# Tying later weight conversions behind one another, and reordering early loads, in an attention and two-FFN kernel

## The chip, the cores and the metric

The kernel runs on one core of a Trainium2 chip. The metric is the device time of one execution in microseconds (us); the time given for a kernel is the median of several runs. A core has a matmul engine (PE, with its weight loads shown as PEld), three engines for element-wise work (DVE, ACT and POOL), and SP, which here only issues DMAs. Every engine works through its own list of instructions in the order in which the program wrote it, and waits on semaphores for what other engines or DMAs bring. PE's clock has two levels, 1.2 and 2.4 GHz; the profile gives the granted share of the higher one.

## The reference

What is computed is windowed attention with a linear bias, followed by two feed-forward networks, all in float32:

```python
def _attn_ref(q, k, v):                       # (4, 8, 576, 64) each
    scores = scale * np.matmul(q, k.transpose(0, 1, 3, 2))
    bias = slopes[:, None, None] * (-np.abs(rel))[None]
    mask = (rel >= 0) & (rel < 128)
    scores = np.where(mask, scores + bias[None], -1e9)
    scores = scores - np.max(scores, axis=-1, keepdims=True)
    attn = np.exp(scores)
    attn = attn / (np.sum(attn, axis=-1, keepdims=True) + 1e-09)
    return np.matmul(attn, v)

def _moe_ref(x, w_in, w_out):                 # 2304 x 512, 512 x 2048, 2048 x 512
    h = x @ w_in
    return (h * (1.0 / (1.0 + np.exp(-1.702 * h)))) @ w_out

def _moe2_ref(x, w_gate, w_val, w_out):       # 512 x 1536 twice, 1536 x 512
    g = x @ w_gate
    return (g * (1.0 / (1.0 + np.exp(-g))) * (x @ w_val)) @ w_out
```

The output of each stage is the input of the next. The weights arrive as 64-bit words.

## The kernel before

The 2304 tokens form 18 tiles of 128, in five blocks of 4, 2, 4, 4 and 4 tiles. For each block the kernel runs attention (scores, row minima, exponentials, normalisation, transposes, values), then the first network (W1, that is `w_in` and `w_out`, in 16 chunks of 128 hidden features), and writes the result to DRAM. The second network follows for all tokens at 538 us of the span.

**W1.** Chunk c comes by two DMAs of 512 KB (`load_w`, L186) into a tile `wraw`, which holds 64-bit words. `split_steps` turns it into a high and a low float32 part in five instructions: ACT scales the upper words into `cv` (L197), DVE shifts the lower words in place (L199), DVE joins both (L201), ACT copies the high part into `wt` (L206), and DVE subtracts to get the low part (L208). L199 depends on nothing but the landing of its chunk. `cv` has two buffers.

A matmul by W1 is three: high by high, high by low, low by high (L554 to L556). For chunk f of block j, `h_steps` makes `hp` (12 matmuls), then ACT's tanh (L575), DVE's product (L577), ACT's high part `gh` (L583) and DVE's low part `gl` (L585); `y_part` multiplies these by the chunk's `w_out`, 12 matmuls into four banks `y`.

**What sets the order.** The first part of the program is written out by hand: `PLAN` is a list of tokens, and inside `tc.manual_schedule` PE, DVE, ACT and POOL take the instructions in that order. It covers attention of blocks 0 and 1, W1's chunks 0 to 8 (tokens w0 to w4, in the order 0, 1, 2, 5, 3, 4, 6, 7, 8) and chunks 0 to 7 of block 0's first network. What follows the plan is placed by a scheduler, which may move an instruction ahead into the planned stretch where it depends on nothing there. After the plan block 1 goes through all 16 chunks, then block 0 through chunks 8 to 15; chunks 9 to 15 are converted by `split_next`, called from the loop over `seq`, one chunk for every two of block 1's.

**Loads.** All are issued by SP in one order: q, k and v of block 0 (`load_full`), chunks 0 to 7 of W1, q, k, v of the first two head pairs of block 1 (`load_pair`, tiles `qr`, `kr`, `vr`), then, as buffers come free, chunks 8 to 15 and the other pairs. Chunks 12 to 15 take over buffers that block 1's attention frees. The raw words of `w_gate` and the other weights of the second network are fetched by `fetch` (L250) and prepared in the gaps of the first network (`preparation`, `in_order`); `in_order` queues each of these steps behind the instructions held in `marks`, by an edge of order within one engine, with no semaphore.

Tile names carry numbers in the lists of instructions below: `wraw_132`, `135`, `138`, `141`, `144`, `147` are chunks 0 to 5, `548`, `551`, `554`, `557` chunks 8 to 11, and `1041`, `1044`, `1047`, `1050` chunks 12 to 15. Chunks 6 and 7 are `150` and `153` before, `164` and `167` after.

## Time and profile before

| what | value |
|---|---|
| median of 3 runs | 934.69 us (931.45 to 935.67) |
| the profiled execution, its own time | 936.22 us |
| its span in the profile | 934.3 us |
| mean granted clock of PE | 0.989 |
| PE, DVE, ACT, POOL busy | 904.1, 676.8, 452.2, 117.3 us |

The span runs from the first to the last record of the profile; 1.9 us of the execution's time lie around it. A row of a timeline gives start, duration, engine, line, operation, output and input; a bracket at its end gives the idle time of that engine just before, and what ended it. A row of a table of windows gives, for each engine, the time that it was busy in that stretch and, behind x, the number of its instructions. Matmul durations overlap, so the spacing of starts is what a matmul costs.

### The profile page before, as it was taken

What the parts mean: (1) busy time and instruction counts of PE and PEld (TensorE: products, weight loads), DVE (VectorE), ACT (ScalarE), POOL (GpSimd) and SP (SyncE); (2) the same over time, 40 slices, a digit from 0 to 9 for tenths busy, and PEclk for the clock granted to TensorE, in tenths of its full rate; (3) what the DMA queues carried; (4) which work ended last, traced back from release to release, by engine and by line L of the source; (5) the groups of instructions that cost most, each with busy time, mean ns of one, the idle gap of its engine ahead of it and who ended that gap; (6) DMA issues with size and microseconds to landing.
All of it is one profiled execution on the core that took longest, in us unless ns stands there. A gap on an engine that the chain in (4) does not pass through costs nothing.

```text
span 934.3 us, 15603 instructions
## 1 busy us (share of the span) xinstructions
PE 904.1 (97%) x5572; PEld 801.1 (86%) x5572; DVE 676.8 (72%) x1716; ACT 452.2 (48%) x1052; POOL 117.3 (13%) x221
## 2 busy tenths in 40 slices
PE   6779999999999999999999999999999999999998
PEld 4456898777777877778888899999999999999998
DVE  7668685676676667766647668899976679866777
ACT  5645474554465446554434445545444435344331
POOL 4632102331233003230000000000000000000000
PEclk9979999999999999999999999999999999999999
DMA  9943311344654445434563587999897667887763
GB/s 327 343 178 105 119 47 34 115 159 140 217 196 161 155 173 186 139 125 174 201 234 114 214 325 282 319 351 340 323 342 283 247 238 242 281 298 249 262 243 136
DMA packets 72461, 201.30 MB, mean 215 GB/s; under 512 B 6848, under 2 KB 38080, under 8 KB 65472
## 3 DMA queue, kind: packets, MB, share of 16 engines
q1 hardware_dynamic: 72384, 200.31, 60.3%
q8 instruction: 44, 0.72, 0.3%
q14 instruction: 33, 0.27, 0.1%
HBM read 156.76 MB, written 43.52 MB: 214 GB/s over the span
## 4 chain that ended last, share of the span: by engine, by line
PE 87%; DMA 8%; DVE 2%; SPq 1%; ACT 1%; issue 0%; POOL 0%; DVEq 0%; ACTq 0%
PE sx L705 15%; PE ox L705 8%; PE sz L705 8%; PE hp L554 7%; PE y L554 7%; PE hp L556 7%; PE hp L555 7%; PE y L555 7%; PE y L556 6%; PE sy L705 4%; PE oz L705 4%; DMA wraw<-in_moe_w_out 4%; PE xb L507 2%; PE sb L354 2%; PE oy L705 2%; PE pt L446 1%
## 5 line engine op out<-in xcount | busy, mean ns | idle before, releaser
L705 PE MATMUL sx<-ya,wg 128*128 128x384 f32 x864 | 172.2, 336 | 1.2 <-DMA wg<-w_scratch 1.0
L705 PEld LDWEIGHTS sx<-ya,wg 128*128 128x128 f32 x864 | 151.6, 188 | 2.1 <-DMA wg<-w_scratch 2.0
L554 PE MATMUL hp<-xh,wt 128*128 128x512 f32 (+1 forms) x320 | 122.2, 382 | 1.5 <-DVE stat L379 1.4
L556 PE MATMUL hp<-xh,wt 128*128 128x512 f32 (+1 forms) x320 | 119.7, 374 | 0.3 <-DVE wt L208 0.3
L555 PE MATMUL hp<-xl,wt 128*128 128x512 f32 (+1 forms) x320 | 119.6, 374 | 0.0
L555 PE MATMUL y<-gl,wt 128*128 128x512 f32 (+1 forms) x320 | 117.9, 372 | 0.0
L556 PE MATMUL y<-gh,wt 128*128 128x512 f32 (+1 forms) x320 | 117.4, 371 | 0.0
L554 PE MATMUL y<-gh,wt 128*128 128x512 f32 (+1 forms) x320 | 113.6, 378 | 1.2 <-DVE yt L618 0.6
L414 POOL TENSOR_SCALAR prob<-prob,stat 128x128 f32<-128x128 f32 x144 | 67.6, 488 | 214.4 <-DVE stat L408 129.1
L585 DVE TENSOR_TENSOR gl<-th,gh 128x512 fp32r<-128x512 f32 (+1 forms) x80 | 51.9, 648 | 57.7 <-ACT gh L583 56.8
L705 PE MATMUL ox<-p,wg 128*128 128x384 f32 x432 | 89.7, 337 | 0.7 <-DMA wg<-wo_scratch 0.7
L705 PE MATMUL sz<-ya,wg 128*128 128x384 f32 x432 | 88.0, 336 | 0.0
L734 DVE TENSOR_TENSOR p<-th,p 128x384 fp32r<-128x384 f32 x126 | 68.2, 553 | 25.0 <-ACT p L733 24.2
L583 ACT ACTIVATE gh<-th 128x512 fp32r<-128x512 f32 (+1 forms) x80 | 46.8, 585 | 72.2 <-PE y L556 58.5
L733 ACT ACTIVATE p<-th 128x384 fp32r<-128x384 f32 x126 | 63.7, 521 | 35.1 <-DVE th L729 24.9
L705 PEld LDWEIGHTS ox<-p,wg 128*128 128x128 f32 x432 | 76.5, 188 | 1.0 <-DMA wg<-wo_scratch 1.0
L705 PEld LDWEIGHTS sz<-ya,wg 128*128 128x128 f32 x432 | 76.0, 188 | 0.1
L395 ACT ACTIVATE prob<-prob,stat 128x128 f32<-128x128 f32 x144 | 56.2, 392 | 39.4 <-DVE stat L379 39.4
L554 PEld LDWEIGHTS hp<-xh,wt 128*128 128x128 f32 x320 | 61.3, 192 | 14.5 <-issue 3.1
L556 PEld LDWEIGHTS hp<-xh,wt 128*128 128x128 f32 x320 | 61.3, 192 | 11.7 <-DVE wt L208 0.8
L554 PEld LDWEIGHTS y<-gh,wt 128*128 128x128 f32 x320 | 58.1, 188 | 15.0 <-issue 1.8
L555 PEld LDWEIGHTS hp<-xl,wt 128*128 128x128 f32 x320 | 61.4, 192 | 9.9
(94 smaller groups left out, 1535.9 us busy)
## 6 DMA issues: line engine op xcount, KB each, us to landing
wg<-w_scratch SPq DMA_DIRECT2D x36, 1024.0 KB, 5.2
wg<-w_scratch SPq DMA_DIRECT2D x36, 768.0 KB, 6.4
wg<-wo_scratch SPq DMA_DIRECT2D x18, 1024.0 KB, 6.4
wg<-wo_scratch SPq DMA_DIRECT2D x18, 768.0 KB, 8.1
w_scratch<-wa SPq DMA_DIRECT2D x24, 512.0 KB, 2.7
w_scratch<-wb SPq DMA_DIRECT2D x24, 384.0 KB, 3.2
wraw<-in_moe_w_in SPq DMA_DIRECT2D x16, 512.0 KB, 8.5
wraw<-in_moe_w_out SPq DMA_DIRECT2D x16, 512.0 KB, 8.8
```

The lines of the kernel that those rows point to most:

```text
L354: nc.tensor.matmul(out=sb[e][c : c + size, (i % 2) * 256 + lo : (i % 2) * 256 + hi], lhsT=u["q"][rows, i * P + c : i * P + c + size], rhs= ...
L395: nc.scalar.activation(out=prob[:, x], in_=prob[:, x], func=AF.Exp, bias=stat[:, 0, x : x + 1], scale=-1.0, accum_out=stat[:, 1, x : x + 1],)
L414: (nc.vector if (j, hp, g) in NORM_ON_VECTOR else nc.gpsimd).tensor_scalar(out=prob[:, x], in0=prob[:, x], scalar1=stat[:, 3, x : x + 1], ...
L507: nc.tensor.matmul(out=x[r][e * D : (e + 1) * D, i * P + a : i * P + a + w], lhsT=u["v"][e][keys, kt + lead, :], rhs=u["pf"][keys].rearran ...
L554: nc.tensor.matmul(out=out_ap, lhsT=whi, rhs=xhi, start=start, stop=False)
L555: nc.tensor.matmul(out=out_ap, lhsT=whi, rhs=xlo, start=False, stop=False)
L556: nc.tensor.matmul(out=out_ap, lhsT=wlo, rhs=xhi, start=False, stop=stop)
L583: a = nc.scalar.activation(out=gh[:, :m], in_=th[:, :m], func=AF.Copy)
L585: d = nc.vector.tensor_tensor(out=gl[:, :m], in0=th[:, :m], in1=gh[:, :m].bitcast(F32), op=ALU.subtract)
L705: nc.tensor.matmul(out=bank_[:, :HT], lhsT=w[:, kk, at, a, :], rhs=p2[2 * (q // 2 - 1) + kk, i][:, b, :] if m == "O" else y2[q // NP2, i][ ...
L733: nc.scalar.activation(out=t[:, 0], in_=src, func=AF.Copy)
L734: nc.vector.tensor_tensor(out=t[:, 1], in0=src, in1=t[:, 0].bitcast(F32), op=ALU.subtract)
```

## The change

`split_next` now opens an edge of order behind `marks["w"]`, the last L208, for every chunk it converts: each DVE instruction of a chunk from 9 on stands behind the L208 of the chunk converted before it. Chunk 8, still in the plan, is the first of that row. SP loads six chunks of W1 ahead of block 1's first two pairs, not eight, and the other two behind them. Since `load_w` now leaves its DMA in `marks["s"]`, the first fetch of `w_gate`, which went through `in_order`, is placed behind all loads of W1.

```diff
@@ load_w
-            nc.sync.dma_start(out=t[:, i].rearrange("p c w -> p (c w)"), in_=src.bitcast(U32))
+            marks["s"] = nc.sync.dma_start(out=t[:, i].rearrange("p c w -> p (c w)"), in_=src.bitcast(U32)).ins
@@ split_steps
-        nc.vector.tensor_tensor(out=t[:, :, 1, :], in0=cf, in1=t[:, :, 0, :].bitcast(F32), op=ALU.subtract)
+        marks["w"] = nc.vector.tensor_tensor(
+            out=t[:, :, 1, :], in0=cf, in1=t[:, :, 0, :].bitcast(F32), op=ALU.subtract
+        ).ins
@@ split_next
         for i in range(len(w), min(len(raw), upto)):
-            w[i] = list(split_steps(raw[i]))[-1]
+            with tc.issue_after(marks["w"]):
+                w[i] = list(split_steps(raw[i]))[-1]
@@
-    load_w1(NW1 - 8)
+    load_w1(NW1 - 10)
     for hp in range(2):
         load_pair(1, hp)
+    load_w1(2)
```

The lists of instructions show it at three places. From line 208 on the changed kernel's lines are numbered two to four higher. The first place is DVE in the planned stretch, around the normalisation of block 1's first pair (`stat_497`) and the conversion of chunk 2 (`138`). Before:

```order
L199 TENSOR_SCALAR wraw_138<-wraw_138 128x1024
L199 TENSOR_SCALAR wraw_551<-wraw_551 128x1024
L407 TENSOR_SCALAR stat_497<-stat_497 128x4
L408 RECIPROCAL stat_497<-stat_497 128x4
L543 TENSOR_TENSOR xl_370<-xb_527,xh_369 128x512
L201 SCALAR_TENSOR_TENSOR cv_468<-cv_468,wraw_138 128x1024
L199 TENSOR_SCALAR wraw_147<-wraw_147 128x1024
L543 TENSOR_TENSOR xl_370<-xb_539,xh_369 128x512
L199 TENSOR_SCALAR wraw_557<-wraw_557 128x1024
```

The same place of DVE after:

```order
L199 TENSOR_SCALAR wraw_138<-wraw_138 128x1024
L409 TENSOR_SCALAR stat_497<-stat_497 128x4
L410 RECIPROCAL stat_497<-stat_497 128x4
L545 TENSOR_TENSOR xl_370<-xb_527,xh_369 128x512
L201 SCALAR_TENSOR_TENSOR cv_468<-cv_468,wraw_138 128x1024
L199 TENSOR_SCALAR wraw_147<-wraw_147 128x1024
L545 TENSOR_TENSOR xl_370<-xb_539,xh_369 128x512
```

The shifts of chunks 9 and 11, which no token of the plan asks for there, are gone; those of chunks 10, 12, 13, 14 and 15 left the planned stretch in the same way, seven in all. The second place is DVE at the end of the plan, where block 1's first chunks (`th_1066`, `th_1098`, `th_1142`) begin. Before:

```order
L201 SCALAR_TENSOR_TENSOR cv_1165<-cv_1165,wraw_551 128x1024
L585 TENSOR_TENSOR gl_1032<-th_1025,gh_1031 128x512
L199 TENSOR_SCALAR wraw_548<-wraw_548 128x1024
L577 SCALAR_TENSOR_TENSOR th_1066<-th_1066,hp_1053 128x256
L208 TENSOR_TENSOR wt_1169<-cv_1165,wt_1169 128x2x512
L201 SCALAR_TENSOR_TENSOR cv_1027<-cv_1027,wraw_548 128x1024
L577 SCALAR_TENSOR_TENSOR th_1098<-th_1098,hp_1085 128x256
L585 TENSOR_TENSOR gl_1070<-th_1066,gh_1069 128x256
L201 SCALAR_TENSOR_TENSOR cv_1236<-cv_1236,wraw_554 128x1024
```

The same place of DVE after:

```order
L587 TENSOR_TENSOR gl_1032<-th_1025,gh_1031 128x512
L199 TENSOR_SCALAR wraw_548<-wraw_548 128x1024
L579 SCALAR_TENSOR_TENSOR th_1066<-th_1066,hp_1053 128x256
L579 SCALAR_TENSOR_TENSOR th_1098<-th_1098,hp_1085 128x256
L201 SCALAR_TENSOR_TENSOR cv_1027<-cv_1027,wraw_548 128x1024
L587 TENSOR_TENSOR gl_1070<-th_1066,gh_1069 128x256
L208 TENSOR_TENSOR wt_1037<-cv_1027,wt_1037 128x2x512
L199 TENSOR_SCALAR wraw_551<-wraw_551 128x1024
L626 TENSOR_SCALAR yt_1117<-y_705 128x512
L201 SCALAR_TENSOR_TENSOR cv_1165<-cv_1165,wraw_551 128x1024
L587 TENSOR_TENSOR gl_1102<-th_1098,gh_1101 128x256
```

Two conversions overlapped on DVE before, and now each one's three DVE instructions are done before the next one's begin; the rest of the row of eight goes on in this way, one conversion for about two of block 1's chunks. The third place is SP's list of early loads. Before:

```order
L186 DMA wraw_150<-in_moe_w_in 128x1024
L186 DMA wraw_150<-in_moe_w_out 128x1024
L186 DMA wraw_153<-in_moe_w_in 128x1024
L186 DMA wraw_153<-in_moe_w_out 128x1024
L301 DMA qr_156<-in_q 128x256
L302 DMA kr_157<-in_k 128x384
L304 DMA vr_158<-in_v 128x192 x2
L301 DMA qr_163<-in_q 128x256
L302 DMA kr_164<-in_k 128x384
L304 DMA vr_165<-in_v 128x192 x2
L250 DMA raw_1849<-in_moe2_w_gate 128x2x256 x2
L250 DMA raw_1970<-in_moe2_w_gate 128x2x256 x2
```

The same place of SP after:

```order
L303 DMA qr_150<-in_q 128x256
L304 DMA kr_151<-in_k 128x384
L306 DMA vr_152<-in_v 128x192 x2
L303 DMA qr_157<-in_q 128x256
L304 DMA kr_158<-in_k 128x384
L306 DMA vr_159<-in_v 128x192 x2
L186 DMA wraw_164<-in_moe_w_in 128x1024
L186 DMA wraw_164<-in_moe_w_out 128x1024
L186 DMA wraw_167<-in_moe_w_in 128x1024
L186 DMA wraw_167<-in_moe_w_out 128x1024
L186 DMA wraw_548<-in_moe_w_in 128x1024
L186 DMA wraw_548<-in_moe_w_out 128x1024
```

Block 1's first pairs pass chunks 6 and 7, and the four fetches of `w_gate` leave the place; they now stand behind the last loads of W1. POOL's list is the same in both kernels, ACT's and DVE's differ only between the end of the plan and block 2's attention and at a few neighbours in the second network.

## Rows read from the trace of the kernel before

**Rows 1.** The page's first lines: span, and busy time by engine.

```profile
span 934.3 us, 15603 instructions
PE 904.1 (97%) x5572; PEld 801.1 (86%) x5572; DVE 676.8 (72%) x1716; ACT 452.2 (48%) x1052; POOL 117.3 (13%) x221
```

**Rows 2.** Windows: stretch, length, PE PEld DVE ACT POOL busy, clock, DMA share, GB/s.

```profile
43.80:50.00 6.20, 1.31 (x24) 0.78 (x20) 0.07 (x2) 1.18 (x4) 0.00 (x0) 0.96 1.03 400
50.00:55.00 5.00, 1.63 (x5) 0.89 (x6) 4.75 (x11) 1.06 (x1) 3.48 (x4) 0.50 0.80 310
55.00:60.00 5.00, 5.00 (x14) 3.89 (x14) 4.64 (x19) 2.90 (x10) 1.88 (x3) 0.52 0.02 7
...
83.30:87.30 4.00, 3.97 (x10) 3.08 (x11) 3.42 (x16) 2.56 (x6) 1.67 (x4) 0.57 0.13 51
107.00:136.00 29.00, 28.94 (x218) 27.69 (x217) 27.28 (x38) 23.66 (x36) 0.00 (x0) 1.00 0.19 71
```

**Rows 3.** Timeline of DVE, first wait.

```profile
49.95 0.70 DVE L199 TENSOR_SCALAR wraw<-wraw 128x1024 uint32<-128x1024 uint32 x1 [6.13 <-DMA wraw<-in_moe_w_out]
...
50.76 0.18 DVE L408 RECIPROCAL stat<-stat 128x4 f32<-128x4 f32 x1
...
53.76 0.69 DVE L199 TENSOR_SCALAR wraw<-wraw 128x1024 uint32<-128x1024 uint32 x1
```

**Rows 4.** Timeline of PE, first wait and the matmuls behind it.

```profile
51.56 0.47 PE L446 MATMUL pt<-ident,prob 128*128 128x128 f32 x1 [6.45 <-POOL prob L414]
...
55.79 0.63 PE L556 MATMUL hp<-xh,wt 128*128 128x512 f32 x1
56.22 0.63 PE L554 MATMUL hp<-xh,wt 128*128 128x512 f32 x1
...
59.93 0.39 PE L554 MATMUL hp<-xh,wt 128*128 128x512 f32 x1
60.16 0.39 PE L555 MATMUL hp<-xl,wt 128*128 128x512 f32 x1
```

**Rows 5.** Timeline of POOL: four normalisations, at two places.

```profile
51.13 3.48 POOL L414 TENSOR_SCALAR prob<-prob,stat 128x128 f32<-128x128 f32 x4 [9.59 <-DVE stat L408]
...
84.36 1.67 POOL L414 TENSOR_SCALAR prob<-prob,stat 128x128 f32<-128x128 f32 x4 [14.95 <-DVE stat L408]
```

**Rows 6.** Timeline of DVE, second wait.

```profile
81.03 0.69 DVE L199 TENSOR_SCALAR wraw<-wraw 128x1024 uint32<-128x1024 uint32 x1 [3.05 <-DMA wraw<-in_moe_w_out]
...
82.06 1.22 DVE L208 TENSOR_TENSOR wt<-cv,wt 128x1024 fp32r<-128x1024 f32 x1
```

**Rows 7.** Timeline of PE at the second wait.

```profile
82.28 0.47 PE L554 MATMUL hp<-xh,wt 128*128 128x512 f32 x1 [1.45 <-DVE stat L379]
...
83.33 0.56 PE L556 MATMUL hp<-xh,wt 128*128 128x512 f32 x1 [0.34 <-DVE wt L208]
```

**Rows 8.** Waits by group, 0 to 100 us: us in total, times, longest.

```profile
DVE wraw L199 <- DMA wraw<-in_moe_w_out: 13.4, 4, 6.1
```

**Rows 9.** Timelines of SP (fetches of `w_gate`) and PE (first scores of block 1).

```profile
35.83 2.71 SPq L250 DMA_DIRECT2D raw<-in_moe_w_gate  x4
...
36.40 0.85 PE L354 MATMUL sb<-kr,qr 64*64 64x192 f32 x16 [2.32 <-DMA kr<-in_k]
```

**Rows 10.** Line L219, first reader of `raw`: ns min/median/max, first and last start.

```profile
L219 ACT ACTIVATE cs<-raw x36: 644/663/684, 169.3 to 631.5; 128x512 f32<-128x512 f32 x36
```

**Rows 11.** Groups, DVE and ACT, 107 to 136 us: busy, mean ns | idle.

```profile
L201 DVE SCALAR_TENSOR_TENSOR cv<-cv,wraw 128x1024 uint32<-128x1024 uint32 x8 | 9.7, 1220 | 0.1
L208 DVE TENSOR_TENSOR wt<-cv,wt 128x1024 fp32r<-128x1024 f32 x8 | 9.6, 1218 | 0.5 <-ACT wt L206 0.5
L577 DVE SCALAR_TENSOR_TENSOR th<-th,hp 128x256 f32<-128x256 f32 (+1 forms) x9 | 4.0, 444 | 2.2 <-ACT th L575 2.2
...
L197 ACT ACTIVATE cv<-wraw 128x1024 f32<-128x1024 f32 x8 | 9.1, 1149 | 0.6 <-DVE wt L208 0.6
L206 ACT ACTIVATE wt<-cv 128x1024 fp32r<-128x1024 f32 x8 | 8.4, 1060 | 0.9 <-DVE cv L201 0.8
```

## The prediction

> **What bounds the kernel now.** Over the whole span PE is busy 904.1 of 934.3 us, 97% [rows 1], so only about 30 us can be had from idle time, and what PE loses at the low clock beside it. I read the waits of PE by stretch first: nearly all idle time lies ahead of 100 us, in the planned stretch. The timelines of that stretch then show one sequence with two instances.
>
> The first: DVE shifts chunk 2's words, and next in its list stands the shift of a chunk that the plan doesn't ask for yet, chunk 9. It waits 6.13 us for that chunk's DMA, until 49.95 [rows 3]. Meanwhile nothing else moves: from 43.8 to 50.0 DVE is busy 0.07 us, POOL not at all, PE 1.31, and the DMA engines are full at 400 GB/s [rows 2]. Behind the shift stands the reciprocal that POOL's four normalisations need; POOL starts at 51.13 after 9.59 us without work [rows 5], and PE's transposes after 6.45 idle [rows 4]. So the DMA holds DVE, DVE holds POOL, POOL holds PE, and none of the three needs the chunk. Behind the wait the granted clock is 0.50 from 50 to 55 us and 0.52 from 55 to 60 [rows 2], the lower level, and 512-wide matmuls start 0.43 us apart where they later start 0.23 apart [rows 4].
>
> The second: chunk 13's shift waits 3.05 us, until 81.03, and the low part of chunk 4 (L208), which PE needs next, starts at 82.06 behind it [rows 6]. PE idles 1.45 and 0.34 us [rows 7], and its clock falls again: 0.57 from 83.3 to 87.3, ten matmuls in 4.0 us [rows 2]. Two more such waits, of chunks 12 and 14, are in the total of 13.4 us for four [rows 8]; I count nothing for them, since PE's list of waits has none that ends behind either.
>
> **The change part by part.** (1) The ties. The lists show the shifts of chunks 9 to 15 gone from the planned stretch, all seven, and with them all four waits. An instruction that DVE doesn't hold cannot wait there.
>
> *First wait.* The instructions behind it come earlier by at least the wait, 6.1 us, and by at most the wait and the shift's own 0.70 [rows 3], 6.8. I take PE's idle time, 6.45 [rows 4], rounded to 6.5, since it lies between and is what PE can gain. What is late next is DVE itself: it is busy 4.75 and 4.64 of the next 5 us each [rows 2]. But two more shifts leave that stretch, chunks 11 and 10 with 0.70 each, so that DVE reaches chunk 2's low part about 6.8 + 1.4 = 8.2 us earlier, and PE arrives there 6.5 to 8.8 earlier, by the clock. The two stay together within what can be read here.
>
> *The clock behind it.* PE now has the transposes spread over POOL's 3.5 us instead of a stop of 6.45. If the clock stays up, the matmuls from 55 to 60 us, 5.0 / 0.43 = 11.6 of them, gain 0.20 each: 2.3 us. If it falls as before, 0. I take 2.3, by the nearest row: PE's stop of 2.32 us ahead of 36.40 [rows 9], also among small matmuls, left the clock up, since it is still 0.96 on the mean of 43.8 to 50 [rows 2]. Against this, the clock fell behind the second wait after only 1.8 us idle. Both ends stay in the range.
>
> For the clock the Trainium skill (TensorE: Matmul & The Clock Gate, Part 1: The HAM clock gate) says that the throttled state is the default, and that one kernel showed 6, 11 or 14 slow matmuls at its start in different runs. By those counts, an estimate from that page, the term would be 1.2 to 2.8 us in place of 2.3, and the sum 11.1 to 12.8; this trace's 11.6 lies inside.
>
> *POOL's length.* The four normalisations take 3.48 us beside a full DVE and 1.67 elsewhere [rows 5]. The same instructions of DVE stand beside them after, but for the last, chunk 11's shift at 53.76 [rows 3], so I leave the 3.48 and count nothing; the ends are 0 and, at 1.67 / 4 for the fourth, 0.4 us gained. The Trainium skill (SBUF — State Buffer, section SBUF: two separate sides) says that a DVE instruction with two SBUF inputs or in a two-port mode and a GpSimd instruction exclude each other while they run. By that rule the fourth normalisation, which ended at 54.61, is freed of that shift and the sum is 12.6; the two rows speak for the rule, but no row shows the four with that shift away.
>
> *Second wait.* Both idle times go, 1.45 + 0.34 = 1.8 us, because DVE has the low part of chunk 4 ready: it is rid by then of five shifts, 3.5 us, and of at least 6.13 + 3.05 us of waiting, 12.7 in all, against PE's 8.8. The ten slow matmuls at 0.40 become ten at 0.23: 1.7 us. Its lower end is 0, should the clock fall for another reason.
>
> *Where the shifts went.* They stand now between block 1's chunks, 107 to about 150 us, where PE is full and DVE has 27.28 of 29.00 us [rows 2]. A conversion there costs DVE 0.70 + 1.22 + 1.22 = 3.1 us, and two chunks of block 1 some 4 x 0.45 = 1.8 [rows 11], together 4.9 for every 48 matmuls, which at half of 0.23 take PE 5.5. The tie adds a wait: L208 for the chunk's own L206 on ACT, with `gl` and `th` queued behind it on DVE and PE's `y` behind these. Before, two conversions overlapped and this wait was 0.5 us in all; now it can be up to ACT's 1.06 each [rows 11]. So the bounds are 0 and 8 x (4.9 + 1.06 - 5.5) = 3.7 us lost. I take 0: `y` runs two chunks behind `hp`, and by the lists a converted chunk is wanted eight chunks of block 1 later at first (chunk 9) and two at the end (chunk 15).
>
> (2) *Block 1's q, k, v ahead of two chunks.* PE waited 2.32 us for the first `kr` at 36.40 [rows 9]; with 2 MB less ahead of it, at some 400 GB/s, it comes 5 us sooner. That idle time goes, but POOL, on whose results PE waits next, was at work until 41.5 all the same (9.59 us idle ahead of 51.13 [rows 5]), so I count 0. The ends are 0 and 2.3; I keep 0.7 of it for the range, as DVE too had work meanwhile. Chunks 6 and 7 move back by 1 MB, 2.5 us, and are read forty us later.
>
> (3) *The raw words of `w_gate`* leave SP's list at 35.83, 2.71 us of issuing and 1 MB [rows 9], which lets chunks 8 to 11 land sooner. They are issued behind the last load of W1, near 105 us, and first read at 169.3 [rows 10]: 0.
>
> The sum is 6.45 + 2.3 + 1.79 + 1.7 = 12.2 us. From the profiled execution, 936.22 with a span of 934.3, that gives 924.0 and 922.1; that execution lies 1.5 us above the median of the runs, so the median becomes 934.69 - 12.2 = **922.5 us**.
>
> **The rivals.** *The clock falls all the same.* After the first wait the transposes trickle in behind POOL, and PE may be held at the lower level again when the large matmuls start. For it: the second wait needed only 1.8 us of idling. Against it: the stop ahead of 36.40, which no fall followed. Time: 934.69 - 6.5 - 1.8 - 1.7 = 924.7.
>
> *DVE is the next bound.* It was 93 to 95% busy behind the first wait [rows 2]; if it doesn't keep up with PE at the higher clock, the clock terms and the second idle time come back as short waits of PE for `wt` and `th`. Against it: 1.4 us of shifts leave that stretch. Time: 934.69 - 6.5 = 928.2.
>
> *The tied row binds block 1, and the kernel is slower.* If ACT has the next chunk's L197 (1.15) and a pair of small copies (0.8) ahead of each L206, DVE stands 3 us at each L208 and one conversion takes 4.9 + 3.0 = 7.9 us, against PE's 5.5 for two chunks. Eight of them lose 19 us, which gives 934.69 - 12.2 + 19 = 941.5. It decides from 7.6 us per conversion: there 8 x 2.1 us eat the gain and 4.7 more. Against it: the next L197 may start when L208 frees its `cv` buffer, and runs while DVE is at the following shift and join, 1.9 us; and DVE's work in that stretch rises by only six shifts, 4 us.
>
> *It doesn't do what it says.* The edge is one of order, and the scheduler could put another unready instruction in the gap. The lists show none; 934.7.
>
> **How the numbers follow.** Forecast 55%, clock 25%, DVE bound 11%, slower 4%, nothing 5%. About 0.5%, 4.7 us, is what a measurement of this kernel can tell from no change: faster below 930.0, slower above 939.4. The first three cases are all faster: 0.88 after the part of the third that runs into 930; same 0.08; slower 0.04. The range goes down to 13.5 us gained (the upper ends 6.8, 0.4 and 0.7) and 1.7 more for the spread of a median, 919.5, and up to the third case, 928.5.
>
> **What would show it.** DVE's waits for W1's DMA gone between 43 and 100 us; POOL's normalisations of block 1's first pair near 44.5; the first `hp` near 48.5; a granted clock of 1.0 from 50 us; chunk 4's matmuls without idle time near 71; PE full from there, `hp` of block 1 starting near 95. Wrong would be idle time of PE behind `y` or `hp` between 95 and 140, or L208 waiting for L206 by 2 us and more each.

## The result, and the profile after

The changed kernel takes 926.4 us, the median of five runs (924.2 to 926.9), against 934.7; the ratio is 0.9907, 95% interval 0.9886 to 0.9928. It is faster by 8.3 us. The forecast was 922.5 us with a range of 919.5 to 928.5: the direction and the range hold, the gain was put 4 us too high. Two repeats, shown below, give 0.9898 and 0.9907; over all 15 timed runs the median is 925.4, and over 55 of the kernel before 934.1.

The profiled execution took 924.2 us with a span of 922.3, so 12.0 us less than the profiled one of before (936.2), where the prediction's sum is 12.2. That agreement is luck: cut at one instruction, as below, this pair gained 15.4 us early and lost 3.4 behind. Why the medians differ by less is the main question of what follows. The page's first lines, which answer to [rows 1]:

```profile
span 922.3 us, 15619 instructions
PE 903.9 (98%) x5572; PEld 800.8 (87%) x5572; DVE 679.8 (74%) x1716; ACT 451.6 (49%) x1052; POOL 116.9 (13%) x221
```

The same five windows as in [rows 2], with the same columns (the changed kernel is further on in its program in each):

```profile
43.80:50.00 6.20, 6.20 (x48) 4.97 (x45) 5.50 (x20) 3.79 (x11) 2.68 (x3) 1.00 0.98 364
50.00:55.00 5.00, 5.00 (x31) 3.65 (x30) 4.65 (x8) 4.20 (x7) 2.76 (x4) 1.00 0.35 98
55.00:60.00 5.00, 5.00 (x25) 4.18 (x24) 4.30 (x7) 4.04 (x6) 1.95 (x2) 1.00 0.46 179
83.30:87.30 4.00, 4.00 (x19) 3.29 (x18) 1.51 (x1) 0.81 (x1) 1.21 (x2) 1.00 0.26 89
107.00:136.00 29.00, 29.00 (x251) 27.92 (x249) 25.41 (x50) 18.31 (x34) 0.00 (x0) 1.00 0.06 22
```

Where PE was busy 1.31 of 6.20 us it is now full, and the clock is 1.00 in all five. The list of DVE's waits between 30 and 150 us (total, times, longest) has no wait for W1's DMA any more, where [rows 8] had 13.4 us:

```profile
DVE wt L208 <- ACT wt L206: 5.2, 8, 2.2
DVE xl L545 <- ACT xh L553: 5.2, 4, 3.9
DVE gl L587 <- ACT gh L585: 4.3, 7, 1.3
DVE th L579 <- ACT th L577: 3.2, 3, 2.2
```

The tied row's own wait, L208 for L206, rose from 0.5 us [rows 11] to 5.2 for eight. On DVE's timeline the reciprocal stands directly behind chunk 2's shift, at 41.93 instead of 50.76 [rows 3]:

```profile
40.91 0.69 DVE L199 TENSOR_SCALAR wraw<-wraw 128x1024 uint32<-128x1024 uint32 x1
41.72 0.17 DVE L409 TENSOR_SCALAR stat<-stat 128x4 f32<-128x4 f32 x1
41.93 0.18 DVE L410 RECIPROCAL stat<-stat 128x4 f32<-128x4 f32 x1
```

POOL's four normalisations follow at once, and take 2.90 us, not 3.48 [rows 5]:

```profile
42.30 2.90 POOL L416 TENSOR_SCALAR prob<-prob,stat 128x128 f32<-128x128 f32 x4 [2.38 <-DVE stat L410]
```

PE's timeline: no stop ahead of the transposes, the first `hp` at 45.42 instead of 54.79, and chunk 2's first matmul at 52.12 at the higher clock (0.23 us apart from there). The last three rows are the new waits of the stretch behind.

```profile
38.68 5.71 PE L521 MATMUL xb<-pf,qkv 128*64 128x256 f32 x32 [1.83 <-POOL pf L476]
44.31 0.76 PE L356 MATMUL sb<-kr,qr 64*64 64x192 f32 x16
45.01 0.66 PE L448 MATMUL pt<-ident,prob 128*128 128x128 f32 x4
45.42 0.48 PE L556 MATMUL hp<-xh,wt 128*128 128x512 f32 x1
...
52.12 0.50 PE L556 MATMUL hp<-xh,wt 128*128 128x512 f32 x1
...
104.12 0.39 PE L557 MATMUL y<-gl,wt 128*128 128x256 f32 x1 [0.37 <-DVE gl L587]
...
157.89 0.47 PE L556 MATMUL hp<-xh,wt 128*128 128x512 f32 x1 [0.49 <-DVE stat L381]
...
170.74 0.47 PE L556 MATMUL y<-gh,wt 128*128 128x512 f32 x1 [1.03 <-DVE stat L381]
```

PE's waits behind 500 us (total, times, longest) all lie in the second network, which starts at 530.6 us in the trace of before, not at 538, and at 516.6 in the changed kernel. First in the kernel before, 1.7 us in all:

```profile
PE sx L705 <- DMA wg<-w_scratch: 1.0, 1, 1.0
PE ox L705 <- DMA wg<-wo_scratch: 0.7, 1, 0.7
```

and in the changed kernel, 3.7:

```profile
PE ox L707 <- DMA wg<-wo_scratch: 1.7, 1, 1.7
PE sx L707 <- DMA wg<-w_scratch: 1.1, 2, 0.9
PE sx L707 <- ACT pc L722: 0.9, 1, 0.9
```

So the gain is made ahead of 100 us and partly given back behind. For the comparisons I cut each trace at one instruction that all have, the 77th matmul of `hp` (101.39 us in the first trace of before, 86.04 here): **early** is the time to its start, **rest** the device time less early.

### The profile page after: what moved, and what is told of

Same layout as the page of the kernel before. It is cut to its first block, busy times and chain, and to the rows that moved or that the text cites. A ratio compares the mean times of both kernels' runs of the same rounds, so it can differ in the third digit from the quotient of the medians.

```text
span 922.3 us, 15619 instructions
## 1 busy us (share of the span) xinstructions
PE 903.9 (98%) x5572; PEld 800.8 (87%) x5572; DVE 679.8 (74%) x1716; ACT 451.6 (49%) x1052; POOL 116.9 (13%) x221
## 4 chain that ended last, share of the span: by engine, by line
PE 87%; DMA 5%; DVE 4%; ACT 1%; POOL 1%; issue 1%; SPq 1%; DVEq 0%; ACTq 0%; POOLq 0%
PE sx L707 15%; PE ox L707 8%; PE sz L707 7%; PE hp L556 7%; PE y L556 7%; PE hp L558 7%; PE hp L557 7%; PE y L557 7%; PE y L558 7%; PE oz L707 4%; PE sy L707 4%; PE sb L356 2%; PE xb L509 2%; PE oy L707 2%; PE xb L521 1%; PE pt L448 1%
## 5 line engine op out<-in xcount | busy, mean ns | idle before, releaser
L556 PE MATMUL hp<-xh,wt 128*128 128x512 f32 (+1 forms) x320 | 120.8, 377 | 0.9 <-DVE stat L381 0.5
L558 PE MATMUL hp<-xh,wt 128*128 128x512 f32 (+1 forms) x320 | 118.3, 370 | 0.0
L585 ACT ACTIVATE gh<-th 128x512 fp32r<-128x512 f32 (+1 forms) x80 | 46.9, 587 | 74.9 <-PE y L558 61.2
L556 PEld LDWEIGHTS hp<-xh,wt 128*128 128x128 f32 x320 | 60.3, 188 | 13.8 <-issue 2.5
L557 PEld LDWEIGHTS y<-gl,wt 128*128 128x128 f32 x320 | 60.3, 189 | 11.4 <-issue 1.0
L556 PEld LDWEIGHTS y<-gh,wt 128*128 128x128 f32 x320 | 57.7, 188 | 14.2 <-issue 3.5
L558 PEld LDWEIGHTS y<-gh,wt 128*128 128x128 f32 x320 | 60.3, 189 | 11.0 <-issue 1.0
```

What stands on the lines that cost most here:

```text
L556: nc.tensor.matmul(out=out_ap, lhsT=whi, rhs=xhi, start=start, stop=False)
L557: nc.tensor.matmul(out=out_ap, lhsT=whi, rhs=xlo, start=False, stop=False)
L558: nc.tensor.matmul(out=out_ap, lhsT=wlo, rhs=xhi, start=False, stop=stop)
L585: a = nc.scalar.activation(out=gh[:, :m], in_=th[:, :m], func=AF.Copy)
```

## The experiments

Each kernel's time is a median, with the ratio to the kernel before run beside it. The runs come from several chips, on which the medians of the kernel before are 933.7 to 934.7 us. The numbers of the traces, in us (fills are the small matmuls without use of e7_fills; "slow" is the number of 512-wide matmuls of W1 that took 0.55 us or more ahead of 70 us and behind, where they take 0.39 at the higher clock):

| trace | device time | first hp | early | rest | slow |
|---|---|---|---|---|---|
| before, first | 936.2 | 54.8 | 101.4 | 834.8 | 11 + 9 |
| e8_before | 937.5 | 54.9 | 101.7 | 835.7 | 11 + 8 |
| e9_before2 | 933.2 | 53.5 | 98.3 | 834.9 | 10 + 0 |
| e10_before3 | 935.5 | 56.1 | 100.4 | 835.1 | 7 + 0 |
| changed, first | 924.2 | 45.4 | 86.0 | 838.2 | 0 |
| e1_again | 925.3 | 46.5 | 87.2 | 838.1 | 0 |
| e12_again2 | 926.5 | 47.9 | 88.5 | 838.0 | 0 |
| e2_ties | 924.8 | 47.9 | 88.6 | 836.3 | 0 |
| e3_loads | 934.3 | 51.8 | 96.4 | 837.9 | 6 + 0 |
| e4_ties_loads | 926.5 | 47.5 | 88.1 | 838.4 | 0 |
| e5_shift9 | 932.8 | 52.1 | 93.9 | 838.9 | 5 + 0 |
| e6_first | 926.4 | 47.4 | 89.0 | 837.5 | 0 |
| e7_fills | 924.2 | 45.6 | 86.2 | 837.9 | 0 |
| e11_first_fills | 923.5 | 46.5 | 88.6 | 834.9 | 0 |

### The ties alone

The ties' edges are kept in a name of their own, so that nothing else follows them; loads are as before.

```diff
+        tied["w"] = nc.vector.tensor_tensor(           # in split_steps, L208
...
+            with tc.issue_after(tied["w"]):            # in split_next
+                w[i] = list(split_steps(raw[i]))[-1]
...
     load_w1(NW1 - 8)
     for hp in range(2):
         load_pair(1, hp)
```

> The ties alone: the loads stand as in the kernel before (eight chunks of W1 ahead of block 1's q, k, v, raw words of w_gate free in their place). Lists of PE, DVE, ACT and POOL are those of the changed kernel. Theory (the tie carries the gain, the loads the rest): all of DVE's waits for W1's DMA between 43 and 100 us are gone, PE's wait of about 2.3 us for the first kr stays near 36, the first hp starts near 48.3 (6.5 earlier than before), against 45.4 with all three parts; time about 929.3 us (927.5 to 930.5). Rival 1 (the order of the loads is what freed DVE): chunk landings are as before, POOL's normalisations stay near 51, time 933 to 936. Rival 2 (the wait for kr is hidden, as the prediction had it, and the first hp came earlier for another reason): first hp near 45.4, time 926.4 (924 to 927).

Measured: 924.5 us (924.2 to 926.1), ratio 0.9895 (0.9880 to 0.9909). The trace is the theory's, the time is rival 2's. PE's timeline shows the wait for `kr` still there, and the first `hp` 6.85 us earlier than in the first trace of before:

```profile
36.48 0.85 PE L356 MATMUL sb<-kr,qr 64*64 64x192 f32 x16 [2.01 <-DMA kr<-in_k]
...
47.50 0.68 PE L448 MATMUL pt<-ident,prob 128*128 128x128 f32 x2 [1.50 <-POOL prob L416]
47.94 0.48 PE L556 MATMUL hp<-xh,wt 128*128 128x512 f32 x1
```

So the ties carry the whole gain in time. The loads bring the first `hp` 0 to 2.5 us forward on top of them (45.4 to 47.9 in three traces of the changed kernel), but most of that is how late an execution starts: DVE shifts chunk 1 at 28.45, 29.35 and 31.00 us in the three, and at 30.34 here. From that shift to the first `hp` it takes 16.9 to 17.2 us in all six traces with ties and reordered loads, 17.6 here and 18.1 in e6_first, which has the old loads too; the loads are worth 0.4 to 1.3 us there. The rest is longer with them (838.1 against 836.3), and no difference in time is left.

### The loads alone

```diff
-    load_w1(NW1 - 8)
+    load_w1(NW1 - 10)
     for hp in range(2):
         load_pair(1, hp)
+    load_w1(2)
```

> The reordered loads alone: block 1's first q, k, v behind six chunks of W1 instead of eight, no tie, raw words of w_gate as before. Lists of all engines but SP are those of the kernel before. Theory: as many bytes stand ahead of chunk 9 as before, so DVE still waits for it until about 50 us and POOL starts near 51; PE's wait for kr near 36 is gone but PE then waits longer behind POOL; first hp at 54.8 within 0.5; time 934.7 us (933 to 936.5). Rival (the wait for kr stands on the path): first hp near 52, time about 931.8. If both e2 and e3 are additive parts of the change, their gains sum to its 8 to 12 us; if the loads pay only behind the ties, e3 gains nothing and e2 falls short of the change by about 3.

Measured: 932.6 us (928.7 to 935.2), ratio 0.9975 (0.9960 to 0.9990): 2.3 us by the ratio. The rival's numbers came true, with the first `hp` at 51.8, but not its reason. Chunk 9's DMA lands sooner, so that DVE's wait for it is 2.52 us and ends 2.96 us earlier than in [rows 3], and POOL, on which PE waits, is still held by DVE:

```profile
46.99 0.69 DVE L199 TENSOR_SCALAR wraw<-wraw 128x1024 uint32<-128x1024 uint32 x1 [2.52 <-DMA wraw<-in_moe_w_out]
...
48.17 3.47 POOL L414 TENSOR_SCALAR prob<-prob,stat 128x128 f32<-128x128 f32 x4 [5.39 <-DVE stat L408]
```

SP issues chunk 9's two DMAs at 37.6 and 38.8 us in this trace, and at 39.8 and 40.2 in the first of before. Why they get through sooner was not tried by itself. The gains do not add: 9.6 us by the ties and 2.3 by the loads make 11.9, where the change has 8.7 over all its runs. What the loads shorten here, DVE's wait for chunk 9, is gone with the ties anyway.

### Without the third part

The change, but the raw words of `w_gate` where they were (the ties' edges are in a name of their own again):

```diff
-            marks["s"] = nc.sync.dma_start(out=t[:, i].rearrange("p c w -> p (c w)"), in_=src.bitcast(U32)).ins
+            nc.sync.dma_start(out=t[:, i].rearrange("p c w -> p (c w)"), in_=src.bitcast(U32))
```

> The change without its third part: raw words of w_gate stay where the scheduler put them before (near 36 us in SP's list), ties and loads as changed. Lists of PE, DVE, ACT and POOL are those of the changed kernel. Theory: nothing on DVE or PE waits for the 1 MB that comes in between, so time 926.4 us (924 to 927.5), first hp near 45.4, no wait of PE for wt; chunks 8 to 11 land about 2.5 us later unseen. Rival: with 1 MB more ahead of them chunks 6 and 7, which now stand behind q, k, v, or block 1's second k, v come too late, and PE stops behind wt or kr: 928 to 930 us with PE idle time behind 50 us.

Measured: 925.6 us (924.3 to 926.5), ratio 0.9901 (0.9888 to 0.9914). The theory holds: the third part is worth nothing that can be measured, and PE waits for no `wt` in the trace. The first `hp`, at 47.5, comes 2 us later than the theory says, as chunk 1's shift does (30.6 us).

### One shift put back

To the ties alone, a token `s:9` adds the shift of chunk 9 where it stood before; the other instructions of chunk 9 stay tied.

```diff
-V:0.2 X:0.3 N:1.0.0 Z:0.3 P:1.0.0
+V:0.2 X:0.3 s:9 N:1.0.0 Z:0.3 P:1.0.0
...
+        if tag not in shifted:                         # in split_steps, ahead of L199
...
+        elif op == "s":
+            words, _, tag = raw1[at[0]]
+            low = words[:, :, :, 0]
+            nc.vector.tensor_scalar(out=low, in0=low, scalar1=29, scalar2=None, op0=ALU.logical_shift_right)
```

> The ties alone (as in e2_ties), but one instruction put back by hand into the planned list: the shift of chunk 9's words, 0.70 us, ahead of the reciprocal of block 1's first pair, where it stood in the kernel before. Everything else of chunk 9 stays tied. Theory (that one row in DVE's list, waiting for a DMA, is the first wait): chunk 9 lands near 50 us as before, DVE waits about 6 us for it, POOL's normalisations start near 51, the first hp near 54.8 instead of 47.9, and the granted clock is at the lower level in 50 to 60 us; the second stop of PE (1.8 us near 82 in the kernel before) does not come back. Time 924.5 + 6.9 + 2.3 = 933.7 us (932 to 935). Rival 1 (the clock does not fall, since the stop is the same but the matmuls behind it come otherwise): 931.4. Rival 2 (the wait is hidden behind something else that the ties moved): first hp within 1 us of 47.9, time 924.5 to 926.

Measured: 932.7 us (930.5 to 935.5), ratio 0.999 (0.9975 to 1.0004). One instruction of 0.69 us in DVE's list takes back 8.2 of the 9.6 us that the ties gain by these medians. The time is the theory's; in this trace the chunk landed some 2 us sooner than in [rows 3], so that the wait was 4.30 us and the first `hp` came at 52.1, not near 54.8:

```profile
47.75 0.69 DVE L902 TENSOR_SCALAR wraw<-wraw 128x1024 uint32<-128x1024 uint32 x1 [4.30 <-DMA wraw<-in_moe_w_out]
48.35 0.16 DVE L410 TENSOR_SCALAR stat<-stat 128x4 f32<-128x4 f32 x1
48.55 0.18 DVE L411 RECIPROCAL stat<-stat 128x4 f32<-128x4 f32 x1
```

PE stops behind POOL again, and the matmuls behind the stop start at the lower clock (five slow ones):

```profile
49.35 0.33 PE L449 MATMUL pt<-ident,prob 128*128 128x128 f32 x1 [3.07 <-POOL prob L417]
51.25 1.17 PE L449 MATMUL pt<-ident,prob 128*128 128x128 f32 x3 [1.57 <-POOL prob L417]
52.07 0.78 PE L557 MATMUL hp<-xh,wt 128*128 128x512 f32 x1
```

The second stop does not come back, as expected: from the first `hp` to the cut this trace needs 41.8 us, the kernels with all ties 40.6, and the four traces of before 44.3 to 46.9.

### The ties of chunks 9 to 11 alone

```diff
-            with tc.issue_after(tied["w"]):
+            with tc.issue_after(tied["w"]) if i < 12 else ExitStack():
```

> The ties of chunks 9, 10 and 11 alone; chunks 12 to 15 stay free, and their shifts stay in the planned stretch; loads as before. Theory (two separate waits, and the loads of chunks 12 to 15 are issued behind PE's xb matmuls, so that they come earlier along with PE): first hp near 47.9 as in e2_ties, at the higher clock, 9 us gained by 65 us; DVE's waits for chunks 12 and 13 stay at 2 to 3 us each, PE stops 1.5 to 2 us near 72 and its clock falls behind that, so 3.5 of the 12.8 us that the ties have gained by 100 us are missing; time 928.0 us (926.5 to 929.5). Rival 1 (chunk 13 lands at its old time, near 81): DVE waits some 10 us for it, PE stops for 6 or more, and the gain is nearly gone: 932 to 934. Rival 2 (with 7 us more in hand DVE is through before PE needs the low part): no stop, 924.5.

Measured: 923.9 us (922.7 to 926.4), ratio 0.9898 (0.9880 to 0.9916). The theory missed by 4 us: rival 2's time. But not for its reason. DVE still waits for chunk 13, and the wait does little harm: from the first `hp` to the cut this trace needs 41.5 us, with all ties 40.6. The scheduler now puts that shift behind chunk 4's low part; [rows 6] have the two the other way round. The shift also stood ahead of a row minimum, which is what ended the longer of PE's two waits in [rows 7]; DVE's row in the trace of before:

```profile
81.64 0.28 DVE L379 CUSTOM_DVE_ANT_0 prob<-sb,bias 128x128 f32<-128x128 f32 x1
```

In e6_first the row minima of that place (L381) are done by 68.9 us, ahead of the shift:

```profile
68.77 1.22 DVE L208 TENSOR_TENSOR wt<-cv,wt 128x1024 fp32r<-128x1024 f32 x1
69.91 0.68 DVE L579 SCALAR_TENSOR_TENSOR th<-th,hp 128x512 f32<-128x512 f32 x1
71.86 0.70 DVE L199 TENSOR_SCALAR wraw<-wraw 128x1024 uint32<-128x1024 uint32 x1 [1.26 <-DMA wraw<-in_moe_w_out]
```

So the second stop was a matter of place as well: a shift that waits costs PE time where something wanted stands behind it, and not elsewhere. Since the order differs, this run says nothing on whether a tie of chunks 12 to 15 is needed at the old place.

### Small matmuls where PE waits

In the changed kernel's first trace the granted clock is 0.65 and 0.68 from 10 to 20 and 20 to 25 us, 1.00 to 35, and 0.69 and 0.63 from there to 40 and to 45: 32 `xb` matmuls take 5.71 us from 38.68. The change with 38 matmuls without use in PE's list:

```diff
-    def values(j, hp):
+    def values(j, hp, fills=0):
...
         x = [bank("xb") for _ in range(2 if quarters else 1)]
+        fill(x[0], fills)
...
-V:0.0
+V:0.0+20
...
-T:0.2.1
+T:0.2.1+6
...
-V:0.3
+V:0.3+12
```

> The changed kernel with 38 small matmuls without use (128x128, some 0.13 us each at the higher clock) in PE's list where it waits in the first 40 us: 20 ahead of the first values' matmuls (block 0, pair 0), 6 ahead of the transposes that wait for POOL near 34, 12 ahead of the values of block 0's last pairs near 37. Theory (the low clock between 10 and 45 us, 0.50 to 0.84 in these stretches, costs time on the path): the clock stays at 1.0 from 20 to 45 us, the 32 xb matmuls that took 5.7 us take 3.2, first hp near 43 instead of 45.4 to 46.5, time 923.0 us (922 to 924). Rival 1 (ahead of 45 us PE waits for POOL and DVE whatever its clock, or what is won is waited for later): first hp within 0.7 of 45.4 to 46.5, time 925.4 (924.3 to 926). Rival 2 (the clock is low all the same, and the fills only take PE's time): first hp at 47 to 49, 926.5 to 928.

Measured: 923.7 us (921.7 to 924.8), ratio 0.9890 (0.9871 to 0.9909). The clock did what the theory says, 1.00 in every window from 10 to 45 us; here three of them (columns as in [rows 2]):

```profile
20.00:25.00 5.00, 4.87 (x43) 3.85 (x44) 4.55 (x23) 5.00 (x18) 3.45 (x8) 1.00 1.03 415
...
35.00:40.00 5.00, 4.91 (x35) 3.76 (x35) 4.42 (x14) 3.28 (x7) 4.86 (x9) 1.00 1.03 416
40.00:45.00 5.00, 4.04 (x50) 2.64 (x46) 4.63 (x14) 2.56 (x7) 2.62 (x4) 1.00 1.04 396
```

and the 32 matmuls take 3.25 us. But the first `hp` is no earlier than in the changed kernel's best trace, since PE then waits for POOL:

```profile
39.74 3.25 PE L522 MATMUL xb<-pf,qkv 128*64 128x256 f32 x32
...
45.18 0.68 PE L448 MATMUL pt<-ident,prob 128*128 128x128 f32 x2 [1.14 <-POOL prob L416]
45.62 0.48 PE L557 MATMUL hp<-xh,wt 128*128 128x512 f32 x1
```

That is rival 1 for the place: from chunk 1's shift to the first `hp` it takes 16.9 us, as without the fills. The time, 923.7, is the theory's; it lies 1.7 us below the changed kernel's pooled median, inside the intervals, and the trace does not show where such a gain would come from.

### The kernels once more

> The changed kernel once more, in more executions, to see why its median (926.4 us) lies 3.9 us above the forecast while its profiled execution (924.2) lies exactly 12.0 below that of the kernel before (936.2). Theory A: the executions differ by where TensorE's granted clock is at the lower level in the first 60 us; the times again fall into two groups, near 924.3 and near 926.6, and a profiled execution of the slower group shows 512-wide matmuls at 0.43 us spacing somewhere between 45 and 60 us, which the profiled one at 924.2 does not have. Rival B: the executions differ by waits for DMA late in the program (behind 530 us); then the first 100 us of a slower execution look as in the faster one, PE starts on the second network at 516.6 in both, and the extra 2 us stand behind sx and ox.

Measured: 925.3 us (924.3 to 925.4), ratio 0.9898 (0.9884 to 0.9912). Theory A fell: no slow 512-wide matmul in the trace. Against rival B, its start was 1.1 us later than in the first trace; but by 492.1 us both stand at the same matmul, and the extra 1.1 us are indeed waits behind `sx` and `ox` (4.8 us against 3.7).

> The kernel before once more, for one more trace of it. Its profiled execution (936.2 us) lies 2.1 us above the median of its runs (934.1), while traces of the kernels with the ties show 2.6 to 4.8 us of PE's waits behind 500 us where that execution shows 1.7. Theory (waits for DMA in the second network vary from execution to execution, and the profiled execution of the kernel before had few of them and a slow start): another execution shows a first hp 1 to 3 us earlier than 54.8, and 2.5 to 4.5 us of waits of PE behind 500 us; time 932.5 to 935. Rival (the new lists or the earlier arrival make the waits in the second network): waits of 1.5 to 2.0 us behind 500 again, first hp at 54.8 within 0.5, time 935 to 936.5.

Measured: 937.5 us, first `hp` at 54.86, 2.1 us of waits behind 500: the rival, in all but the time, which is longer still.

> The kernel before once more, one trace. Its two traces so far (936.2 and 937.5 us) show 1.7 and 2.1 us of PE's waits behind 500 us; six of the seven kernels that come there 5 to 14 us earlier show 3.0 to 4.8, among them the reordered loads alone, whose lists of PE, DVE and ACT are those of the kernel before. Theory A (the waits vary by execution, the two traces had few by chance, and both had a slow start, since the median of its runs is 934.0): a trace with 3 us or more behind 500, or one with its first hp at 52 to 53 us and a shorter wait of DVE for chunk 9. Theory B (they come of the earlier arrival): 1.6 to 2.2 us again.

Measured: 933.2 us, first `hp` at 53.52, 2.0 us of waits: theory B, as far as one trace goes.

> The same once more: four traces of the kernel before tell chance from rule better than three. Theory A: among the four at least one with 3 us or more of PE's waits behind 500 us, and at least one with a first hp earlier than 53.5. Theory B: all four between 1.6 and 2.2 us behind 500.

Measured: 935.5 us, first `hp` at 56.08, 2.9 us of waits. Neither A nor B: one trace of four just misses A's 3 us and exceeds B's 2.2. What the four do show is in the table: the rest is the same within 0.9 us, and the executions differ by the early part, 98.3 to 101.7, for which DVE's first wait lasts 5.7 to 6.9 us and between 7 and 20 matmuls run slow.

> The changed kernel a third time. From the start of the 77th hp matmul (near 100 us in the kernel before) to the end, four traces of the kernel before take 834.8, 834.9, 835.1 and 835.7 us, and two of the changed kernel 838.2 and 838.1: 3 us given back of the 14 that it has won by there, about 1 of it ahead of 505 us and 2 behind, in PE's waits for DMA. Theory (the part behind 505 us is chance of the execution, as 2.6 to 4.8 us in kernels of the same lists suggest): the times again between 924 and 927, and a trace with another sum of waits behind 500 us, 2.5 to 3.5, and a rest of 836 to 837.5. Rival (a lasting cost of the change): 3.6 us of waits or more behind 500 and a rest of 837.8 to 838.5 once more.

Measured: 926.3 us (923.5 to 928.1), ratio 0.9907 (0.9884 to 0.9929). The rest is 838.0 for the third time, as the rival has it, with 3.5 us of waits behind 500, just under its 3.6. Three traces with 838.0 to 838.2 against four of before with 834.8 to 835.7: the longer rest belongs to the changed kernel and is no accident of one execution.

### The best pieces together

The fills, the reordered loads, and ties for chunks 9 to 11 alone.

```diff
-            with tc.issue_after(marks["w"]):
+            with tc.issue_after(marks["w"]) if i < 12 else ExitStack():
```

> The pieces that did best so far together: loads and raw words of w_gate as changed, ties for chunks 9, 10 and 11 alone (chunks 12 to 15 free, as in e6_first), and the 38 small matmuls of e7_fills. Theory (their gains over the changed kernel, some 1 to 1.5 us each, are of different places, the block 1 stretch and the first 40 us, and add): 922.5 us (921 to 924). Rival 1 (what comes earlier is waited for behind 500 us, whatever it is): 924.0 (923.3 to 925.5), as either alone. Rival 2 (chunk 13's shift, free again, waits longer now that DVE comes to it earlier, and PE stops near 70): 926 to 929.

Measured: 922.7 us (922.2 to 923.5), ratio 0.9878 (0.9859 to 0.9897). It is 11.4 us below before by its ratio, and its slowest run lies below the fastest of the changed kernel (923.53), though the two never ran side by side and the intervals of their ratios overlap a little. The theory's sum is met, but the trace puts the gain elsewhere: the early part, 88.6, is no better, and the rest, 834.9, is that of the kernel before. The pair of PE's waits shown above at 157.89 and 170.74 is missing here and in e6_first; all seven traces of kernels that tie chunks 12 to 15 have it (0.5 and 1.0 us, 13 us apart), and none of the seven others.

## Why the prediction was right, and where it was not

**The mechanism was right.** DVE held by a shift that nobody wanted yet, POOL held by DVE, PE held by POOL: one such shift put back undoes the gain (e5_shift9), the ties alone make it (e2_ties), and none of DVE's waits for W1's DMA is left. The four rivals fell: the clock is at its higher level from 46 to 110 us in all traces with all the ties, PE waits for no `wt` or `th` there though DVE is 86 to 93% busy from 50 to 60 us, and the tied row does not bind block 1, since L208's waits reach 2.2 us at most, 0.65 on the mean of eight, and PE is full through 107 to 136 in the first trace. The sign of being wrong that the prediction named, idle time of PE behind `y` or `hp` between 95 and 140, is there in small: 0.37 us at 104.12.

**First wait, 6.45 forecast.** With the ties alone the first `hp` is 6.85 us earlier than in the first trace and 6.9 earlier than the mean of the four. From chunk 1's shift, which leaves out how late an execution starts, it is 7.7 earlier, and 7.1 in e6_first (17.6 and 18.1 against 25.3 on the mean of four), with POOL's shorter work in it. Right, if a little low. In the changed kernel it comes at 45.4 to 47.9, earlier than the 48.5 that I had named as the sign, which is the next point.

**Part (2), 0 forecast.** In the trace a little low, in the time right: the wait for `kr` is gone, and the first `hp` came at 46.6 on the mean of three traces, 1.3 earlier than in the one with the ties alone. From chunk 1's shift it is 0.4 to 1.3, so most of the 2.3 us of that wait was hidden, as the prediction had it. At the end nothing is left of it, since the rest is longer by 1.8.

**POOL's length, 0 forecast with ends 0 and 0.4.** The four normalisations got 0.58 us shorter, beyond the upper end. One of the four takes 1.9 us in every trace. The one beside chunk 11's shift takes 0.88 in the four traces of before and in e3_loads; without that shift, in the nine traces with ties, the other three take 0.36 to 0.38 each. So the rule quoted from the Trainium skill (SBUF — State Buffer, section SBUF: two separate sides) agrees in direction.

**The clock and the second wait, 2.3 + 1.8 + 1.7 = 5.8 forecast.** Against the execution that I sized them on this is exact: from the first `hp` to the cut it took 46.6 us, and every trace with all the ties takes 40.6, 6.0 less. But it was one of the worst of four. The four take 46.6, 46.9, 44.8 and 44.3, on the mean 45.7: the slow matmuls behind the first wait are 11, 11, 10 and 7, and behind the second 9, 8, 0 and 0. The two stops of PE are in all four, their price in clock is not. The second stops that a fall followed were also the longer ones (1.45 and 1.67 us, against 1.01 and 1.17), so chance and length are not told apart here. On the mean the terms are worth 5.0. The Trainium skill (TensorE: Matmul & The Clock Gate, Part 1: The HAM clock gate) says that the number of slow matmuls at the start of one kernel varies from run to run, with 6, 11 and 14 measured. The counts behind the first wait vary in the same way. I had taken such counts as bounds of one number, and sized the term on one execution. One reading was wrong as well: the 1.45 us of the second wait were ended by DVE's row minima [rows 7], not by the low part of chunk 4; both stood behind the same shift, so the term stays.

**Where the shifts went, 0 forecast with 3.7 lost at the other end.** From the cut to the 913th `hp`, near 500 us, the changed kernel takes 405.7 us on the mean of three traces and the kernel before 404.6 on the mean of four: 1.1 lost. PE's waits in that stretch are 2.3 us on the mean of the three against 1.1 of the four. In the first trace they are the new ones at 104, 158, 171 and 344 us. The pair at 158 and 171, 1.5 us, goes with the ties of chunks 12 to 15, as e6_first and e11_first_fills show by lacking it, though e6_first has one of 1.7 us near 225 in its place. The size was inside the bounds that I gave; my choice of 0 was wrong, and so was the place, which I looked for between 107 and 150 us and behind L208.

**What no step had: the second network.** From there to the end the changed kernel takes 432.4 against 430.6, and PE's waits behind 500 us are 4.0 on the mean of three traces against 2.2 of four. This 1.8 us is the term that was missing. By what ended them, 1.0 of it is PE's wait for `wo_scratch`, 0.6 a wait for ACT's `pc`, which the kernel before does not have, and 0.2 the wait for `w_scratch`. I took it that what comes earlier by 100 us is earlier by as much at the end.

**The sum.** By the means of the traces: the first `hp` 8.2 earlier (54.8 to 46.6), the stretch to the cut 5.0 shorter, 1.1 and 1.8 given back: 10.3, from 935.6 to 925.3. The traces of before lie 1.5 above the median of its timed runs. Taking the rest as fixed, the median run of before, 934.1, has its cut at 99.0 and that of the changed kernel, 925.4, at 87.3: 11.7 us gained early, near the 12.2 forecast, and 3.0 given back. So two steps failed. One is the last line of the sum, which took 12.2 us, sized on an execution 1.5 us above the median, off that median; the executions of before differ in the very terms that the change removes, so what lay above the median should have come off the terms. The other is the missing 3.0 us of the rest. That 11.7 comes near 12.2 is luck in part: by the traces the first `hp` gained 1.7 more than its term and the stretch to the cut 0.8 less, and the median execution had 1.5 less to gain. The range holds a small slip: the three upper ends make 13.7 us, not 13.5, so that it would start at 919.3.

**What stays open.** Why PE's waits in the second network grow. Four traces of before have 1.7 to 2.9 us, ten of other kernels 2.6 to 4.8. It is not the ties' order alone: e3_loads, with the lists of before on PE, DVE and ACT, has 3.7 and a rest of 837.9. It is not an earlier arrival alone, as far as one trace shows: e11_first_fills comes to the cut 10 us and more ahead of the kernel before, and has 2.6 and a rest of 834.9. Its waits of PE behind 500 us, all of them (total, times, longest):

```profile
PE sx L708 <- ACT pc L723: 1.7, 1, 1.7
PE ox L708 <- DMA wg<-wo_scratch: 0.9, 1, 0.9
```

None for `w_scratch`. The wait for `pc`, 0.4 to 1.8 us, is in the eight traces that come to the cut by 89.0 us and in none of the six that come at 93.9 or later, so it goes along with an early arrival; no run tests that by itself. The chips are a rival that these traces do not exclude: e11_first_fills ran where e9_before2 and e10_before3 ran, and the changed kernel did not. On the chip of e8_before, with a rest of 835.7, e5_shift9, e6_first and e7_fills have 837.5 to 838.9. The DMA engines' share from 590 to 680 us is 0.93 before and 0.92 in the changed kernel; which transfer is late for what reason was not tried.

## What to carry to other kernels

An engine works through its list in order, so an instruction that waits for data nobody needs yet can cost as much as the wait, whatever its own length: look at what stands behind each long wait, and tie early fillers behind work that is due (here 0.7 us of filler was worth 8 us). Size the terms of a forecast on several executions where the clock is one of them, cut every trace at one instruction, and compare what lies before and behind it: here the early part alone held the spread of the kernel before, and the rest, which the change seemed not to touch, took back a quarter. Where the scheduler is free, check where the neighbours of a moved instruction go; in e6_first the second stop went by a change of place that was not asked for.

## What the runs showed of the hardware

The granted clock of the same program at the same place differs between executions. In four traces of the kernel before, behind stops of PE near 81 us, nine and eight matmuls of the next twelve ran at the lower level in two (stops of 1.45 and 1.67 us), and none in the others (1.01 and 1.17). Behind the first stop, of 6.45, 3.97, 4.44 and 5.53 us, 11, 11, 10 and 7 did. In the changed kernel a wait of 1.83 us ahead of 38.68 was followed by 5.7 us for 32 matmuls in one trace, where [rows 9] show a wait of 2.32 us ahead of 36.40 with no fall behind it. Keeping PE busy with 38 small matmuls held the clock at 1.00 from 10 to 45 us in one trace (e7_fills; in e11_first_fills it was 0.83 from 10 to 20), and gained nothing between chunk 1's shift and the first `hp`, because POOL was the one waited for. A normalisation of 128x128 on POOL took 0.37 us by itself and 0.88 beside a DVE shift of 0.69 us, in five traces. The time at which a chunk of W1 lands also moves: DVE's shift of chunk 9 starts at 48.7, 50.0, 50.0 and 51.3 us in the four traces.
